# A causal convolution, GELU and two matrix products on one core: part of an operand sum goes to DMA, one more block takes Strassen's form

## The chip, the cores and the metric

The kernel runs on one core of a Trainium2 chip. Its engines work side by side and wait for each other by semaphores: TensorE (PE, with its weight loads as PEld), VectorE (DVE), ScalarE (ACT), GpSimd (POOL) and SyncE (SP, which here only issues DMAs). The metric is the device time of one execution in microseconds (us).

## What is computed

The input x has 8 sequences of 4096 tokens with 192 channels, 32768 tokens in all. Each of 8 heads (24 channels) has a causal filter of 7 taps, its weights put through a softmax. The result goes through a two-layer network with 2048 hidden channels and an exact GELU:

```python
w = softmax(weight)                                   # [8 heads, 7 taps]
y[b, s, h, :] = sum_k w[h, k] * x_pad[b, s + k, h, :] # 6 zeros ahead of each sequence
h = y @ w_in                                          # [32768, 192] @ [192, 2048]
out = gelu(h) @ w_out                                 # [32768, 2048] @ [2048, 192], float32
```

## The kernel before

**Tiling.** The tokens are cut into two halves of 16384, one on each half of the 128 partitions. A half is cut into 35 blocks, six of 256 tokens and then 29 of 512 (numbers 6 to 34); a block number stands for that block of both halves. Per block: SP loads x (`load`), DVE transposes it (`trans`, L705), DVE convolves it (`conv`, L726 and L733, with the first tap of some blocks on ACT, L848), PE makes the first product into PSUM (`mm1`, L972), ACT applies GELU into `gT` (L880), PE makes the second product (`mm2_t` L1050, or `mm2_s` L1110 for a Strassen block), the result is transposed by DVE into `osb` (`evac_t` L364, `st_evac` L517), and SP stores it (`store`, L547).

**Stages.** PE's loop over n runs the first product of block n in 16 slices, each of 12 matmuls, and after every slice a share of the second product of block n-1. Matmuls use 64x64 quarters of the array, four at a time; one such group of four with 512 columns is called a round here. A slice of the first product is 3 rounds, a block 48; the second product of a block is 48 rounds too. The first product goes into two PSUM buffers in turn (`hp`), so slice u waits for the GELU of slice u-2.

**Strassen blocks.** For every third block from 9 on (the list `ST`: 9, 12, ..., 30) the second product takes Strassen's form: the two halves of the tokens and pairs of hidden and output columns are a 2x2 matrix of blocks, and sums of operands replace products. It needs 44 rounds (`ROUNDS` says how many after each slice). Its sums of GELU outputs are S1, S3, Dn and S4 (`st_add`, DVE, L454 to L462), each in parts, held in `sst`; S3 is used by the product P7. `st_copy` (ACT, L482) copies partial results out of PSUM in six steps numbered 0 to 5, `st_post` (DVE, L491 to L505) makes five sums of them, `st_evac` transposes the three results. The sums of weights that the form needs are made once by `weights`, L426 to L436.

**What sets the order.** DVE's program is a list of convolution steps per block, with other work put in at places given as (blocks after m, step, order) in `AT_ST` and `at_ev`; DVE works on the convolution of block n+1 while PE is in the first product of block n. ACT's copies stand at (blocks after m, slice) in `AT_COPY`. All engines run their lists strictly in order. SP's loop is: load block n+3, then store block n-1, which waits for that block's last transpose. POOL, after the prologue, has only `halo`: it copies the last 6 tokens of a block ahead of the next block (L632); its DMAs are all in the prologue.

```python
AT_ST = {
    "S1": [(1, 9, 0), (2, 0, 0), (2, 1, 0), (2, 5, -1)],
    "S3": [(2, 0, 1), (2, 5, 1)],
...
AT_COPY = {0: (1, 6), 1: (1, 8), 2: (1, 10), 3: (1, 13), 4: (1, 14), 5: (2, 1)}
```

**The end.** The last block, 34, has no block after it: its second product runs by itself, in four groups g of two matmul chains (L1166). Even groups use PSUM banks that block 33 leaves free (`wait_banks`), odd groups the two `hp` buffers. `evac_half` (L336 on DVE, L338 on ACT) moves each result out, `store_half` stores it.

Of the kernel before, what the change touches and what calls it, by code (L numbers as in the profile page):

```python
# [5 lines left out]
ALU = mybir.AluOpType  # L6
# [5 lines left out]
def bass_lightweight_conv__then__act_gelu_exact_kernel(  # L12
# [58 lines left out]
    M0, M1 = 6, NB - 1  # L71
    ST = [m for m in range(M0 + 3, M1 - 1) if m % 3 == 0]
    K0 = {n: i for i, n in enumerate([4, 5, 6, *(n for n in range(9, NB) if n - 3 not in ST)])}
# [48 lines left out]
    with es:  # L122
# [64 lines left out]
        S_AC = sem("S_AC")  # L187
        S_DP = sem("S_DP")

        block = es.enter_context(nc.Block())  # L190
# [114 lines left out]
        def wait_banks(t, m, g):  # L305

            k = G0[m] + g
            if m < M0:
                if k >= 2:
                    t.wait_ge(S_EVA, k - 1)  # L310
            elif g % 2:
                t.wait_ge(S_GELU, SL0[NB] - 1 + g // 2)
            else:
                t.wait_ge(S_EV, EVC[M1] - 2 + g)
# [94 lines left out]
        def weights(v, k):  # L409

            def b(row, col):
                return ap(wout, row * C + col, [[NF * C, 128], [2 * C, NF // 2], [NP, 64]])

            full = [[NF // 2 * 64, 128], [64, NF // 2], [1, 64]]

            def w(i):
                return ap(wst, i * (NF // 2) * 64, [[4 * NF // 2 * 64, 128], [64, NF // 2], [1, 64]])

            f = ap(wtf, 0, full)
            if k == 0:  # L420
                for i in range(4):
                    v.wait_ge(S_WOUT[i], 16)
            else:
                v.wait_ge(S_WT, k)
            if k == 0:
                ins = v.tensor_tensor(f, b(0, 1), b(0, 0), ALU.subtract)  # L426
            elif k == 1:
                ins = v.tensor_copy(w(0), f)
            elif k == 2:
                ins = v.tensor_tensor(f, f, b(1, 1), ALU.subtract)  # L430
            elif k == 3:
                ins = v.tensor_copy(w(1), f)
            elif k == 4:
                ins = v.tensor_tensor(w(3), b(1, 0), f, ALU.add)
            else:
                ins = v.tensor_tensor(w(2), b(1, 1), b(0, 1), ALU.subtract)  # L436
            ins.then_inc(S_WT)

        PART = {"S1": 4, "S3": 2, "Dn": 2, "S4": 2}

        def st_add(v, m, name, q):
# [11 lines left out]
            if name == "S1":  # L453
                ins = v.tensor_tensor(t(0), a(1, 0), a(1, 1), ALU.add)  # L454
            elif name == "S3":
                ins = v.tensor_tensor(t(1), a(0, 0), a(1, 0), ALU.subtract)
            elif name == "Dn":
                v.wait_ge(S_SA[0], PART["S1"] * i + (q + 1) * n * PART["S1"] // (NF // 2))
                ins = v.tensor_tensor(t(2), a(0, 0), t(0), ALU.subtract)  # L459
            else:  # L460
                v.wait_ge(S_SA[2], PART["Dn"] * i + q + 1)
                ins = v.tensor_tensor(t(3), a(0, 1), t(2), ALU.add)  # L462
            ins.then_inc(S_SA[NS.index(name)])

        def st_copy(a, m, k):
# [6 lines left out]
            if k in (0, 1, 3):  # L472
# [4 lines left out]
                (p5s[LO, 0 : TB // 2], xb(UP, TB // 2)),  # L477
                (uu[LO, :], xb(LO)),
                (gsm[UP, :], uu[LO, :]),
                (uu[UP, :], uu[LO, :]),  # L480
            )[k]
            a.activation(out=dst, in_=src, func=AF.Copy).then_inc(S_AC)  # L482

        def st_post(v, m, k):
# [3 lines left out]
            if k == 0:  # L488
                st_done(v, m, "P7")
                v.wait_ge(S_AC, 6 * i + 2)  # L490
                ins = v.tensor_tensor(tq[UP, :], bank(BK[m]["Y"], UP), p5s[UP, :], ALU.add)  # L491
            elif k == 1:
# [6 lines left out]
            elif k == 3:  # L499
                v.wait_ge(S_AC, 6 * i + 6)  # L500
                v.wait_ge(S_DP, 5 * i + 3)
                ins = v.tensor_tensor(tq[:, :], tq[:, :], uu[:, :], ALU.add)
            else:
                v.wait_ge(S_MM2, MMC[m + 1])
                ins = v.tensor_tensor(gsm[:, :], bank(BK[m]["Y"]), gsm[:, :], ALU.add)  # L505
            ins.then_inc(S_DP)
# [24 lines left out]
        def store(e, m):  # L531
# [30 lines left out]
            "S1": [(1, 9, 0), (2, 0, 0), (2, 1, 0), (2, 5, -1)],  # L562
            "S3": [(2, 0, 1), (2, 5, 1)],
            "Dn": [(2, 0, 2), (2, 5, 2)],
            "S4": [(2, 0, 4), (2, 6, 0)],
            "post": [(2, 11, 0), (3, 0, 0), (3, 2, 0), (3, 6, 0), (3, 6, 1)],
            "ev": [(3, 6, 3), (3, 6, 2), (3, 4, 0)],
        }
# [6 lines left out]

        AT_COPY = {0: (1, 6), 1: (1, 8), 2: (1, 10), 3: (1, 13), 4: (1, 14), 5: (2, 1)}

        @block.gpsimd
        def _(g):
# [71 lines left out]
            halo(2)  # L651
            for n in range(3, NB):
                halo(n)

        @block.vector
        def _(v):
# [117 lines left out]
            for n in range(M0, M1):  # L774
# [3 lines left out]
                else:  # L778
                    for name, ats in AT_ST.items():
                        for q, at in enumerate(ats):  # L780
# [4 lines left out]
                            else:  # L785
                                todo.append((at, st_add, n, name, q))
                side += [((n + at[0], *at[1:]), op, v, *rest) for at, op, *rest in todo]
# [14 lines left out]
        def _(a):  # L802
# [52 lines left out]
            for n in range(NB):  # L855
                w = WS[n]
                for i in range(NSL[n]):
# [26 lines left out]
                    ).then_inc(S_GELU)  # L884

            for g in range(NG[NB - 1]):
                evac_half(a, g, 1)
                store_half(a, g, 1)

        @block.tensor  # L890
        def _(t):
# [182 lines left out]
            def mm2_s(m, e):  # L1074
# [18 lines left out]
                else:  # L1093
                    q = NS.index(src)
                    need(S_SA[q], PART[src] * i + k * PART[src] // (NF // 2) + 1)
                    a, c0 = sst[q], k * TB
# [123 lines left out]
```

## Time and profile before

| | |
|---|---|
| median of 3 runs | 674.67 us (674.18 to 674.76) |
| the profiled execution | 676.39 us, of which span 674.7 us |
| PE busy | 668.8 us (99%) |
| DVE busy | 605.7 us (90%) |
| ACT busy | 584.8 us (87%) |
| POOL busy | 33.1 us (5%) |
| DMA | 53.66 MB, mean 80 GB/s |
| granted PE clock | full speed in every slice of the span |

The span is what the profiler saw from the first to the last instruction; times inside it count from its start. Rows of the timeline give start, duration, engine, line, operation, the tile written and the tile read, shape and count; in square brackets stands how long the engine was idle before, and what ended that. Rows of the waits give who waited for whom, the total in us, how often, and the longest. Rows of a table of stretches give the stretch, its length, the busy time of PE, PEld, DVE, ACT and POOL with the number of instructions, the granted clock, the share of time that the DMA engines were busy, and GB/s. Rows of DMA issues give the number of DMAs, the size of each, and the median us from issue to landing.

### The profile page before, as it was taken

What the parts mean: (1) busy time and instruction counts of PE and PEld (TensorE: products, weight loads), DVE (VectorE), ACT (ScalarE), POOL (GpSimd) and SP (SyncE); (2) the same over time, 40 slices, a digit from 0 to 9 for tenths busy, and PEclk for the clock granted to TensorE, in tenths of its full rate; (3) what the DMA queues carried; (4) which work ended last, traced back from release to release, by engine and by line L of the source; (5) the groups of instructions that cost most, each with busy time, mean ns of one, the idle gap of its engine ahead of it and who ended that gap; (6) DMA issues with size and microseconds to landing.
All of it is one profiled execution on the core that took longest, in us unless ns stands there. A gap on an engine that the chain in (4) does not pass through costs nothing.

```text
span 674.7 us, 27139 instructions
## 1 busy us (share of the span) xinstructions
PE 668.8 (99%) x12504; PEld 418.6 (62%) x12504; DVE 605.7 (90%) x697; ACT 584.8 (87%) x653; POOL 33.1 (5%) x61
## 2 busy tenths in 40 slices
PE   8999999999999999999999999999999999999998
PEld 7999655556555555655565555556555655555557
DVE  5979999899999999999999999999999999998311
ACT  7899988889888988988898889888889988898773
POOL 7000000000000000000000000000000000000000
PEclk9999999999999999999999999999999999999999
DMA  8435234214443043433134431334431344411123
GB/s 146 115 85 142 60 73 90 63 41 96 96 96 81 20 94 96 96 83 85 33 88 96 95 88 22 89 92 95 94 86 31 80 96 95 89 28 47 32 50 94
DMA packets 133282, 53.66 MB, mean 80 GB/s; under 512 B 126384, under 2 KB 133104, under 8 KB 133168
## 3 DMA queue, kind: packets, MB, share of 16 engines
q1 hardware_dynamic: 129136, 49.37, 32.0%
q0 software_dynamic: 2912, 1.97, 2.0%
q8 instruction: 98, 1.61, 1.0%
q10 hardware_dynamic: 1120, 0.59, 0.3%
q14 instruction: 16, 0.13, 0.1%
HBM read 28.31 MB, written 25.17 MB: 79 GB/s over the span
## 4 chain that ended last, share of the span: by engine, by line
PE 93%; ACT 5%; DMA 1%; issue 0%; SPq 0%; DVE 0%; POOL 0%; POOLq 0%; ACTq 0%
PE hp L972 47%; PE ob L1050 31%; PE ob L1110 9%; PE ob L1012 5%; ACT gT L880 4%; DMA xin<-in_x_dram 1%; PE ob L1166 1%; PE hp L1166 1%; ACT gsm L482 1%; ACT uu L482 1%; PE ob L914 0%; DMA wsb<-in_weight_dram 0%; SPq L527 0%; PE ob L972 0%; POOL xTb L265 0%
## 5 line engine op out<-in xcount | busy, mean ns | idle before, releaser
L880 ACT ACTIVATE gT<-hp 128x1024 bf16<-128x1024 f32 x510 | 517.6, 1022 | 74.6 <-PE hp L972 67.7
L972 PE MATMUL hp<-xc,win 64*64 64x512 bf16 (+2 forms) x6036 | 417.6, 366 | 1.0
L733 DVE SCALAR_TENSOR_TENSOR acc<-xT,wcol,acc 128x1024 f32<-128x1024 f32 (+1 forms) x330 | 298.1, 959 | 10.8 <-ACT acc L848 10.8
L972 PEld LDWEIGHTS hp<-xc,win 64*64 64x64 bf16 (+1 forms) x6036 | 192.1, 106 | 128.2 <-ACT gT L880 4.9
L1050 PE MATMUL ob<-gT,wout 64*64 64x512 bf16 x3840 | 261.7, 376 | 0.0
L1050 PEld LDWEIGHTS ob<-gT,wout 64*64 64x64 bf16 x3840 | 123.5, 118 | 87.3
L1110 PE MATMUL ob<-gT,wout 64*64 64x512 bf16 x768 | 97.2, 376 | 0.0
L1110 PE MATMUL ob<-sst,wst 64*64 64x512 bf16 x384 | 79.1, 376 | 0.0
L364 DVE STREAM_TRANSPOSE osb<-ob 128x512 f32<-128x512 f32 x60 | 49.9, 872 | 32.5 <-PE ob L1050 32.5
L705 DVE STREAM_TRANSPOSE xT<-xin 128x1536 f32<-128x1536 f32 (+2 forms) x39 | 74.5, 1920 | 0.9 <-DMA xin<-in_x_dram 0.6
L733 DVE SCALAR_TENSOR_TENSOR xc<-xT,wcol,acc 128x1024 bf16<-128x1024 f32 (+1 forms) x66 | 61.9, 960 | 0.3
L1110 PEld LDWEIGHTS ob<-gT,wout 64*64 64x64 bf16 x768 | 43.5, 118 | 22.2
L632 POOL COPY xT<-xT 128x18 f32<-128x18 f32 x30 | 19.7, 655 | 508.9 <-DVE xc L733 284.7
L848 ACT ACTIVATE acc<-xT,wcol 128x512 f32<-128x512 f32 (+1 forms) x63 | 43.7, 693 | 0.0
L1012 PE MATMUL ob<-wout,gT 64*128 64x192 bf16 x768 | 41.6, 243 | 0.0
L1012 PEld LDWEIGHTS ob<-wout,gT 64*128 64x128 bf16 x768 | 34.2, 94 | 4.2
L1110 PEld LDWEIGHTS ob<-sst,wst 64*64 64x64 bf16 x384 | 32.2, 107 | 5.4
L1110 PE MATMUL ob<-gT,wst 64*64 64x512 bf16 x128 | 35.3, 376 | 0.0
L1110 PE MATMUL ob<-sst,wout 64*64 64x256 bf16 x256 | 27.4, 269 | 0.0
L454 DVE TENSOR_TENSOR sst<-gT 128x1024 bf16<-128x1024 bf16 x32 | 22.0, 688 | 5.4 <-ACT gT L880 5.4
L1110 PEld LDWEIGHTS ob<-sst,wout 64*64 64x64 bf16 x256 | 21.8, 119 | 2.1
L459 DVE TENSOR_TENSOR sst<-gT,sst 128x2048 bf16<-128x2048 bf16 x16 | 19.4, 1216 | 0.0
(73 smaller groups left out, 221.5 us busy)
## 6 DMA issues: line engine op xcount, KB each, us to landing
out_dram<-osb SPq DMA_DIRECT2D x124, 192.0 KB, 3.2
xin<-in_x_dram SPq DMA_DIRECT2D x116, 192.0 KB, 4.0
xin<-in_x_dram SPq DMA_DIRECT2D x18, 96.0 KB, 2.6
wout<-in_moe_w_out_dram POOLq DMA_DIRECT2D x4, 192.0 KB, 4.6
win<-in_moe_w_in_dram POOLq DMA_DIRECT2D x4, 96.0 KB, 4.5
win<-in_moe_w_in_dram POOLq DMA_DIRECT2D x2, 192.0 KB, 5.2
xin<-in_x_dram POOLq DMA_DIRECT2D x4, 96.0 KB, 4.4
out_dram<-osb ACTq DMA_DIRECT2D x4, 96.0 KB, 2.2
```

The source lines that it names most:

```text
L364: v.transpose(osb_t(m, j), bank(BK[m][j])).then_inc(S_EV)
L454: ins = v.tensor_tensor(t(0), a(1, 0), a(1, 1), ALU.add)
L459: ins = v.tensor_tensor(t(2), a(0, 0), t(0), ALU.subtract)
L632: g.tensor_copy(dst, src).then_inc(S_HALO)
L705: v.transpose(out, src).then_inc(S_TR)
L733: ins = v.scalar_tensor_tensor(dst, src, wk, a, op0=ALU.mult, op1=ALU.add)
L848: a.activation(out=acc[n % 2][:, p * TB : p * TB + w], in_=ap(xT[n % 2], p * XW + HX, [[NP * XW, 128], [1, w]]), func=AF.Copy, scale=wcol[ ...
L880: a.activation(out=ap(gT[n % 2], i * c * 2 * w, dst), in_=ap(ob, 2 * TB, [[4 * TB, 128], *src[1:]]) if u < SL0[1] and u % 3 == 2 else ap(h ...
L972: ins = t.matmul(hbuf(u, slice(fo, fo + fw), o, w), ap(win, f1, [[NP * F, 64], [2, fw]]), xc[n % 2][r, p * TB : p * TB + w], start=(p == 0 ...
L1012: ins = t.matmul(bb[sub], gT[m % 2][r, c0 : c0 + 128], wout[r, CH[sub][i] * C : (CH[sub][i] + 1) * C], start=(ph == 0 and k == 0), stop=(p ...
L1050: ins = t.matmul(bank(BK[m][j], slice(64 * h, 64 * h + 64), w), ap(wout, 64 * hf * NF * C + CH[h][i] * C + j, [[NF * C, 64], [NP, 64]],), ...
L1110: ins = t.matmul(bank(BK[m][bk], slice(64 * cg, 64 * cg + 64), w), wt_, a[r, c0 : c0 + w], start=(e == mine[0]), stop=(e in (mine[-1], GRO ...
```

## The change

Signs are changed so that S3 is a plain sum of two GELU outputs, a(0,0) + a(1,0). Three of its four quarters are then made by DMA, issued from POOL: a copy of the first operand within SBUF, and an accumulating DMA of the second operand on top. The copy of quarter q waits for the GELU slices that make it, the accumulate for the copy. The last quarter stays with DVE. The other signs (Dn, three of the weight sums, one of the sums after the product, the scale of ACT copies 4 and 5) follow from that. Copies 4 and 5 of ACT change their order and places, the last sums and transposes of a Strassen block move to later steps, and block 33 joins the Strassen list, with the waits of the last block's second product and of ACT's end set for it. In the diff, `M1` is 34.

```diff
-    ST = [m for m in range(M0 + 3, M1 - 1) if m % 3 == 0]
+    ST = [m for m in range(M0 + 3, M1) if m % 3 == 0]
...
+        S_CP = [sem("S_CP%d" % q) for q in range(3)]
+        S_AD = [sem("S_AD%d" % q) for q in range(3)]
...
         def wait_banks(t, m, g):
...
+            elif M1 - 1 in ST:
+                i = ST.index(M1 - 1)
+                t.wait_ge(*((S_AC, 6 * i + 4) if g == 0 else (S_EV, EVC[M1] - 2)))
+                t.wait_ge(S_DP, 5 * i + 3 + g)
             else:
                 t.wait_ge(S_EV, EVC[M1] - 2 + g)
...
         def weights(v, k):
...
-                ins = v.tensor_tensor(f, b(0, 1), b(0, 0), ALU.subtract)
+                ins = v.tensor_tensor(f, b(0, 0), b(0, 1), ALU.subtract)
...
-                ins = v.tensor_tensor(f, f, b(1, 1), ALU.subtract)
+                ins = v.tensor_tensor(f, f, b(1, 1), ALU.add)
...
-                ins = v.tensor_copy(w(1), f)
+                ins = v.tensor_scalar(w(1), f, -1.0, None, ALU.mult)
...
-                ins = v.tensor_tensor(w(3), b(1, 0), f, ALU.add)
+                ins = v.tensor_tensor(w(3), b(1, 0), f, ALU.subtract)
...
-                ins = v.tensor_tensor(w(2), b(1, 1), b(0, 1), ALU.subtract)
+                ins = v.tensor_tensor(w(2), b(0, 1), b(1, 1), ALU.subtract)
...
-        PART = {"S1": 4, "S3": 2, "Dn": 2, "S4": 2}
+        PART = {"S1": 4, "S3": 4, "Dn": 2, "S4": 2}
+        ND = 3
+
+        def st_dma(e, m, q, h):
+
+            i, n = ST.index(m), NF // 2 // PART["S3"]
+            dst = ap(sst[1], q * n * TB, [[NF // 2 * TB, 128], [TB, n], [1, TB]])
+            src = ap(gT[m % 2], (4 * q * n + h) * TB, [[NF * 2 * TB, 128], [4 * TB, n], [1, TB]])
+            if h == 0:
+                e.wait_ge(S_GELU, SL0[m] + 2 * (q + 1) * n - 1)
+                e.dma_start(dst, src).then_inc(S_CP[q], 16)
+            else:
+                e.wait_ge(S_CP[q], 16 * (i + 1))
+                e.dma_start(dst, src, accum_op=ALU.add).then_inc(S_AD[q], 16)
...
         def st_add(v, m, name, q):
...
-                ins = v.tensor_tensor(t(1), a(0, 0), a(1, 0), ALU.subtract)
+                ins = v.tensor_tensor(t(1), a(0, 0), a(1, 0), ALU.add)
...
-                ins = v.tensor_tensor(t(2), a(0, 0), t(0), ALU.subtract)
+                ins = v.tensor_tensor(t(2), a(0, 0), t(0), ALU.add)
...
         def st_copy(a, m, k):
...
-                (gsm[UP, :], uu[LO, :]),
                 (uu[UP, :], uu[LO, :]),
+                (gsm[UP, :], uu[LO, :]),
             )[k]
-            a.activation(out=dst, in_=src, func=AF.Copy).then_inc(S_AC)
+            a.activation(out=dst, in_=src, func=AF.Copy, scale=-1.0 if k > 3 else 1.0).then_inc(S_AC)
...
         def st_post(v, m, k):
...
-                ins = v.tensor_tensor(tq[UP, :], bank(BK[m]["Y"], UP), p5s[UP, :], ALU.add)
+                ins = v.tensor_tensor(tq[UP, :], bank(BK[m]["Y"], UP), p5s[UP, :], ALU.subtract)
...
-                v.wait_ge(S_AC, 6 * i + 6)
+                v.wait_ge(S_AC, 6 * i + 5)
                 v.wait_ge(S_DP, 5 * i + 3)
...
                 v.wait_ge(S_MM2, MMC[m + 1])
+                v.wait_ge(S_AC, 6 * i + 6)
...
-            "S3": [(2, 0, 1), (2, 5, 1)],
+            "S3": [(2, 5, 1)],
...
-            "post": [(2, 11, 0), (3, 0, 0), (3, 2, 0), (3, 6, 0), (3, 6, 1)],
-            "ev": [(3, 6, 3), (3, 6, 2), (3, 4, 0)],
+            "post": [(2, 11, 0), (3, 0, 0), (3, 2, 0), (3, 6, 0), (3, 9, 0)],
+            "ev": [(3, 10, 0), (3, 7, 0), (3, 4, 0)],
...
-        AT_COPY = {0: (1, 6), 1: (1, 8), 2: (1, 10), 3: (1, 13), 4: (1, 14), 5: (2, 1)}
+        AT_COPY = {0: (1, 6), 1: (1, 8), 2: (1, 10), 3: (1, 13), 4: (2, 1), 5: (2, 4)}
...
         @block.gpsimd
         def _(g):
...
-            for n in range(3, NB):
-                halo(n)
+            for n in range(3, M1 + 2):
+                if n < NB:
+                    halo(n)
+                if n - 2 in ST:
+                    for q, h in ((0, 0), (1, 0), (0, 1), (2, 0), (1, 1), (2, 1)):
+                        st_dma(g, n - 2, q, h)
...
         @block.scalar
         def _(a):
...
+            for k, (d, at) in AT_COPY.items():
+                if NB - d in ST:
+                    st_copy(a, NB - d, k)
...
             def mm2_s(m, e):
...
-                    need(S_SA[q], PART[src] * i + k * PART[src] // (NF // 2) + 1)
+                    part = k * PART[src] // (NF // 2)
+                    if src == "S3" and part < ND:
+                        need(S_AD[part], 16 * (i + 1))
+                    elif src == "S3":
+                        need(S_SA[q], i + 1)
+                    else:
+                        need(S_SA[q], PART[src] * i + part + 1)
```

More of the change, by code (lines that the diff above doesn't have):

```diff
@@ L478, in st_copy @@
                 (uu[LO, :], xb(LO)),
+                (uu[UP, :], uu[LO, :]),
                 (gsm[UP, :], uu[LO, :]),
-                (uu[UP, :], uu[LO, :]),
             )[k]
-            a.activation(out=dst, in_=src, func=AF.Copy).then_inc(S_AC)
+            a.activation(out=dst, in_=src, func=AF.Copy, scale=-1.0 if k > 3 else 1.0).then_inc(S_AC)
         def st_post(v, m, k):
@@ L785, in _ @@
                             else:
-                                todo.append((at, st_add, n, name, q))
+                                todo.append((at, st_add, n, name, q if name != "S3" else ND))
                 side += [((n + at[0], *at[1:]), op, v, *rest) for at, op, *rest in todo]
```

## The prediction

> **What bounds the kernel now.** I read the page's busy times first, then the table of stretches with one row per block, then the list of waits, then ScalarE's timeline where PE waits, then the DMA issues.
>
> ```profile
> PE 668.8 (99%) x12504; PEld 418.6 (62%) x12504; DVE 605.7 (90%) x697; ACT 584.8 (87%) x653; POOL 33.1 (5%) x61
> ```
>
> PE is the bound. A block is 96 rounds of four 64x64 tiles (48 for the first product, 48 for the second), a Strassen block 92. The stretches below begin at first-product slice 0 of blocks 9, 10, 11 and 12; block 9 is in Strassen's form, so its second product runs in the second row.
>
> ```profile
> 127.05:147.77 20.72, 20.72 (x389) 11.83 (x384) 20.04 (x24) 17.89 (x20) 0.20 (x1) 1.00 0.35 78
> 147.77:167.92 20.15, 20.04 (x388) 12.27 (x380) 19.92 (x21) 18.41 (x22) 0.72 (x1) 1.00 0.36 81
> 167.92:188.67 20.75, 20.75 (x386) 11.80 (x389) 20.05 (x23) 18.46 (x21) 1.19 (x1) 1.00 0.35 79
> 188.67:209.39 20.72, 20.72 (x390) 11.77 (x385) 20.03 (x24) 17.89 (x20) 0.20 (x1) 1.00 0.33 78
> ```
>
> Columns: stretch, its length, then busy time of PE, weight loads, DVE, ACT, POOL, granted clock, DMA share. A round is 20.72/96 = 0.2158 us, the clock is full, and 92 rounds should take 19.86. The Strassen stretch took 20.15 and the next 20.75: 0.29 + 0.03 = 0.32 us lost per Strassen block. The waits name the loser, and the timeline the place.
>
> ```profile
> DVE acc L733 <- ACT acc L848: 10.8, 14, 2.4
> DVE sst L454 <- ACT gT L880: 5.4, 8, 0.7
> PEld hp L972 <- ACT gT L880: 4.9, 9, 0.6
> ```
>
> ```profile
> 164.68 0.58 ACT L482 ACTIVATE uu<-ob 64x512 f32<-64x512 f32 x1
> 165.16 1.01 ACT L880 ACTIVATE gT<-hp 128x1024 bf16<-128x1024 f32 x1
> 166.19 0.63 ACT L482 ACTIVATE gsm<-uu 64x512 f32<-64x512 f32 x1
> 166.84 3.00 ACT L880 ACTIVATE gT<-hp 128x1024 bf16<-128x1024 f32 x3
> ...
> 167.92 0.36 PEld L972 LDWEIGHTS hp<-xc,win 64*64 64x64 bf16 x12 [0.59 <-ACT gT L880]
> ```
>
> Two copies on two successive slices push the GELUs back until PE finds its PSUM buffer still unread at 167.92. The 0.59 includes the gap that weight loads have anyway; the loss is the 0.32. DVE, at about 60.0 us in the 61.62 us of three blocks, is nearly full but ahead: block 12's convolution ends at 183.30 and PE wants it at 188.67.
>
> **The change part by part.** The sum goes against the profiled execution (676.39 us, span 674.7); its time is 1.72 over the median 674.67, and I carry the difference over to the median.
>
> *The moved ScalarE copy.* Copies 4 and 5 of a Strassen block leave slice 14 of the next block and slice 1 of the one after for slices 1 and 4 of the one after, at 0.63 each, and swap their order. In the first of the two, without the copy at 14, GELU 14 runs 166.17 to 167.19 and PE wants slice 0 of the next block 5 rounds (3 of slice 15, 2 of the second product) after 166.56, at 167.64: 0.45 to spare, the stall goes. What is late next? The copy at slice 1 runs 169.55 to 170.18, GELU 1 ends 171.25, PE wants slice 3 at 171.55: 0.30 spare, as now (0.29). The copy at slice 4 makes GELU 4 end 175.13 against slice 6 at 175.65: 0.5 spare. So 8 x 0.32 = 2.5 us are gained. DVE's op that needs copy 4 stood at 170.57, 0.4 after the copy; late, it would cost DVE tenths out of its 5.4 us lead.
>
> *Block 33 in Strassen's form.* 20.72 - 19.86 = 0.86 us gained, in the last first-product stage, with the copies placed as above. Behind it, in old times: the last GELU ends 662.23, two copies end 663.5, ScalarE's first eviction waited until 664.37 anyway. DVE does 0.69 + 0.89 + 0.69 of sums and transpose from 662.9, so the Y bank is read by 665.2; PE's third final group, which now waits for it, started at 666.81: 1.6 spare. The last transpose ends 665.9 instead of 663.2, SP's four stores follow until 668.3, and the last output is evicted at 672.29. Nothing on the path.
>
> *DVE work removed.* Two 128x2048 sums per Strassen block (1.20 each) become one 128x1024 (0.69, by the row of that shape): 1.72 us less. DVE is off the path: worth 0 to PE. The weights' signs change, six operations as before; the scale of -1 on a copy changes no operation's shape.
>
> *The six transfers per Strassen block*, three copies and three accumulates of 256 KB, SBUF to SBUF, on POOL's queue. Before shows no such transfer. POOL's queue stands still in these waits; behind them is only the halo copy of block m+3. The one of block 12, at 137.87 now, would come near 148; the transpose that needs it runs at 165.27: 17 us of cover. The last copy waits for the 11th GELU (142.34), the last accumulate for that copy; PE needs the third quarter at round 12 of the Strassen stretch, 153.60. The nearest rows are POOL's own transfers:
>
> ```profile
> wout<-in_moe_w_out_dram POOLq DMA_DIRECT2D x4, 192.0 KB, 4.6
> win<-in_moe_w_in_dram POOLq DMA_DIRECT2D x4, 96.0 KB, 4.5
> win<-in_moe_w_in_dram POOLq DMA_DIRECT2D x2, 192.0 KB, 5.2
> out_dram<-osb ACTq DMA_DIRECT2D x4, 96.0 KB, 2.2
> ```
>
> They ran with the DMA engines 0.80 busy. Here the queues are empty until the next stores:
>
> ```profile
> 142.30:150.90 8.60, 8.60 (x168) 4.90 (x160) 8.60 (x11) 7.65 (x9) 0.00 (x0) 1.00 0.01 3
> ```
>
> At 4.6 each: copy landed 147.0, accumulate landed 151.6, 2.0 us before PE asks. At 5.2: 152.8, 0.8 before. The accumulate has no row. Lower end: 2.2, no loss either way (it can't gain, PE waits for nothing else there). Upper end: twice 5.2, since it reads two operands: from 147.0 it lands at 157.4, 3.8 us late, nine times 34 us. I take 4.6 to 5.2, nearest by queue and size, so no loss. Loss starts at an accumulate of 6.6 us.
>
> [...]
>
> Could POOL's six issues (about 0.7 each) hold DVE? A 64x768 DVE copy took 0.58 beside an issue and 0.42 without: six cost 1.0. The other end, each blocking DVE fully: 4.2. I take 1.0: DVE at 60.0 - 1.7 + 1.0 = 59.3 in 61.30.
>
> *Output transposes spread out.* The last one of a Strassen block moves behind four convolution steps, ending near 177.1 instead of 173.4. SP's store waits for it, and the load queued behind that store moves too: landing 183.3 becomes 187.0, and the transpose that wants it at 185.83 waits 1.2 us on DVE. Its convolutions end at 199.4 and 222.9, PE wants them at 209.4 and 229.5: hidden by over 6 us. Without that lead it would cost 1.2 x 8. The sum that frees the Y bank moves with them, from 171.9 to about 175.6; the bank's next writer is the second product of block 11, from 188.7. The one wait more per quarter on PE (three DMA semaphores and one of DVE's in place of two) I cost at nothing: rounds that wait on semaphores now keep the 0.2158 step.
>
> Sum: 2.5 + 0.86 = 3.4 us off; 676.4 becomes 673.0 profiled, 674.7 becomes **671.3** as median.
>
> **The rivals.**
> 1. *The accumulate lands late* (slower). Place: the third quarter's wait at round 12. It decides from a landing of 7.0 us, where (7.0 - 6.6) x 9 eats the gain. At 7.5, halfway from 4.6 to the upper end, 8.1 lost: 679.4. For: two operands, one queue in order. Against: idle DMA engines. 0.14.
> 2. *The stall only moves*: ScalarE, one copy more in the following block, stalls PE by as much as before, and only block 33 counts: 673.8, within 0.2%. For: 0.30 us spare at slice 3. Against: that is what is spare today. 0.10.
> 3. *DVE becomes the bound*: each issue blocks it fully, 60.0 - 1.7 + 4.2 = 62.5 against 61.30, 1.2 x 8 = 9.6 lost: 680.9. Against: the 0.58 beside 0.42. 0.05.
>
> **How the numbers follow.** Measurement tells about 0.2% (1.35 us) from no change: faster is under 673.3, slower over 676.0. The forecast has 0.71 and its own range 670.4 to 672.6 (a spare time misjudged by 0.1 us, eight times, and 0.4 at the tail). Faster 0.71, same 0.10, slower 0.14 + 0.05 = 0.19. The range begins at 670.3 and takes in rival 2 and an accumulate of up to 7.3 us: 671.3 + 0.7 x 9 = 677.6. Past it lie most of rival 1 and rival 3, and 2 or 3 in 100 of the forecast: under 2 in 10.
>
> **What would show it.** Right: the Strassen stretch at 19.9, its follower at 20.7, no wait of weight loads on GELU with 0.6; a last first-product stage of 19.9; the accumulates landing under 6.6 us after issue; DVE near 58 to 59 us per three blocks. Wrong: PE waiting for a DMA into the sum buffer some four slices into the Strassen stretch; DVE rows grown beside POOL issues; a new wait on GELU at slice 3 or 6 of the following block.

## The result, and the profile after

| | before | after |
|---|---|---|
| median of 4 runs each, on one chip | 674.42 us (673.85 to 674.76) | 670.93 us (670.6 to 671.28) |
| ratio, 95% interval | | 0.9949 (0.9932 to 0.9966) |
| the profiled execution | 676.39 us, span 674.7 us | 670.93 us, span 669.2 us |

The kernel became 3.5 us faster; 3.4 was forecast. The two profiled spans differ by 5.5 us, more than the medians, because the prologues of these two executions differ: the first product of block 6 begins at 69.85 in the one and at 67.72 in the other, 2.13 us that are no part of the change. What remains lies in two places. The eight cycles of three blocks from the first slice of block 9 on took 492.92 us and now take 490.45: 2.47 us. The stage of the last first product, block 34 beside the second product of block 33, took 20.83 and now takes 19.97: 0.86 us. The stretches between are equal, and the tail behind that stage is 13.1 us long in both. In this document, medians and ratios leave out executions over 1.5% slower than the fastest of the same kernel: one of 1007.15 us (mean clock 0.66) of the kernel with the transfers alone, and two, of 732.5 and 735.0, of the kernel whose third copy waits for all 16 GELUs, whose trace is of the first of these two.

The page of the changed kernel: busy times, the chain that ended last, three groups.

```profile
PE 665.8 (99%) x12504; PEld 416.2 (62%) x12504; DVE 604.7 (90%) x703; ACT 587.8 (88%) x659; POOL 91.9 (14%) x115
...
PE 99%; ACT 0%; DVE 0%; DMA 0%; issue 0%; ACTq 0%
...
L652 POOL COPY xT<-xT 128x18 f32<-128x18 f32 x30 | 28.9, 964 | 330.9 <-DVE xc L757 171.3
...
L455 POOL DMA_DIRECT2D sst<-gT x27 | 19.8, 733 | 175.1 <-ACT gT L904 175.1
...
L458 POOL DMA_DIRECT2D sst<-gT x27 | 33.1, 1227 | 8.0 <-DMA sst<-gT 7.9
```

PE alone makes the chain now. In the three groups, POOL spends 0.73 us on issuing a copy and 1.23 on issuing an accumulate, and its halo copies, 0.655 us each before, take 0.964.

The table of stretches of the changed kernel: blocks 9 to 12 one by one, the three blocks from 9 on together, and the last first-product stage. The columns are as in the prediction: length, busy time of PE, weight loads, DVE, ACT and POOL, granted clock, DMA share, GB/s.

```profile
124.92:145.64 20.72, 20.72 (x389) 11.77 (x384) 19.80 (x23) 17.89 (x20) 6.21 (x7) 1.00 0.73 147
145.64:165.50 19.86, 19.86 (x388) 12.28 (x384) 18.50 (x21) 17.90 (x21) 0.72 (x1) 1.00 0.41 90
165.50:186.22 20.72, 20.72 (x388) 11.77 (x384) 19.84 (x23) 19.04 (x22) 1.19 (x1) 1.00 0.34 79
186.22:206.94 20.72, 20.72 (x388) 11.77 (x384) 20.39 (x24) 17.89 (x20) 6.23 (x7) 1.00 0.71 147
...
124.92:186.22 61.30, 61.30 (x1156) 35.82 (x1152) 58.14 (x65) 54.82 (x61) 8.12 (x9) 1.00 0.50 105
...
636.09:656.06 19.97, 19.97 (x388) 12.16 (x381) 6.62 (x9) 18.01 (x21) 0.00 (x0) 1.00 0.22 50
```

The Strassen stretch is 92 rounds of 0.2158 us, 19.86, with nothing lost; its follower is 20.72. DVE has 58.14 us of work in the 61.30 of the three blocks.

ScalarE's timeline of the changed kernel, across the place where PE used to stall:

```profile
161.63 1.02 ACT L904 ACTIVATE gT<-hp 128x1024 bf16<-128x1024 f32 x1 [0.27 <-PE hp L999]
162.55 0.58 ACT L501 ACTIVATE uu<-ob 64x512 f32<-64x512 f32 x1
163.02 2.00 ACT L904 ACTIVATE gT<-hp 128x1024 bf16<-128x1024 f32 x2
165.29 2.10 ACT L904 ACTIVATE gT<-hp 128x1024 bf16<-128x1024 f32 x2 [0.27 <-PE hp L999]
167.42 0.63 ACT L501 ACTIVATE uu<-uu 64x512 f32<-64x512 f32 x1
...
171.31 0.63 ACT L501 ACTIVATE gsm<-uu 64x512 f32<-64x512 f32 x1
```

Only one copy is left among the last slices of the Strassen stretch. The two GELUs behind it end at 165.02, PE begins the next block at 165.50: 0.48 us to spare, where PE used to wait. The two later copies stand at 167.42 and 171.31; PE's slices 3 and 6 of that block then have 0.29 and 0.50 us to spare.

The waits of the changed kernel that replaced the one on GELU (of which one of 0.2 us is left), and the row of DMA issues for the new transfers:

```profile
DVE xT L729 <- DMA xin<-in_x_dram: 9.3, 8, 1.9
POOL sst L458 <- DMA sst<-gT: 7.9, 9, 1.3
DVE acc L757 <- ACT acc L872: 7.3, 12, 1.8
```

```profile
sst<-gT POOLq DMA_DIRECT2D x54, 256.0 KB, 4.1
```

DVE waits for a load eight times, 1.2 us each on average; PE waits for none of it. The last issues of block 9's transfers on POOL's timeline of the changed kernel:

```profile
140.51 0.73 POOL L455 DMA_DIRECT2D sst<-gT  x1 [3.44 <-ACT gT L904]
141.22 1.25 POOL L458 DMA_DIRECT2D sst<-gT  x1
143.26 1.19 POOL L458 DMA_DIRECT2D sst<-gT  x1 [0.79 <-DMA sst<-gT]
144.00 0.83 POOL L652 COPY xT<-xT 128x18 f32<-128x18 f32 x1
```

The third quarter's copy, issued at 140.51, landed 2.46 us later by the semaphore it sets; the accumulate was issued at 143.26 and landed at 148.88. PE asks for it at 151.47: 2.6 us to spare. Over the nine blocks this accumulate took 3.6 to 5.6 us, median 3.9; the 5.6 of block 9 is the longest, the next is 4.2.

### The profile page after: what moved, and what is told of

Its sections match the earlier page's. It is cut to its first block, busy times and chain, and to the rows that moved or that the text cites. A ratio compares the mean times of both kernels' runs of the same rounds, so it can differ in the third digit from the quotient of the medians.

```text
span 669.2 us, 27224 instructions
## 1 busy us (share of the span) xinstructions
PE 665.8 (99%) x12504; PEld 416.2 (62%) x12504; DVE 604.7 (90%) x703; ACT 587.8 (88%) x659; POOL 91.9 (14%) x115
## 4 chain that ended last, share of the span: by engine, by line
PE 99%; ACT 0%; DVE 0%; DMA 0%; issue 0%; ACTq 0%
PE hp L999 49%; PE ob L1077 29%; PE ob L1143 13%; PE ob L1039 5%; PE ob L1199 1%; PE hp L1199 1%; PE ob L941 0%; DMA wsb<-in_weight_dram 0%; PE ob L999 0%; ACT dg L846 0%; DVE wcol L701 0%; ACT xc L237 0%; DVE wnm L692 0%; ACT osb L344 0%; ACT wex L833 0%
## 5 line engine op out<-in xcount | busy, mean ns | idle before, releaser
L1143 PE MATMUL ob<-sst,wst 64*64 64x512 bf16 x432 | 88.9, 376 | 0.0
L652 POOL COPY xT<-xT 128x18 f32<-128x18 f32 x30 | 28.9, 964 | 330.9 <-DVE xc L757 171.3
L370 DVE STREAM_TRANSPOSE osb<-ob 128x512 f32<-128x512 f32 x57 | 47.6, 874 | 4.0 <-PE ob L1077 3.7
L455 POOL DMA_DIRECT2D sst<-gT x27 | 19.8, 733 | 175.1 <-ACT gT L904 175.1
L1143 PEld LDWEIGHTS ob<-sst,wst 64*64 64x64 bf16 x432 | 36.2, 107 | 6.0
L1143 PE MATMUL ob<-gT,wst 64*64 64x512 bf16 x144 | 39.7, 376 | 0.0
L458 POOL DMA_DIRECT2D sst<-gT x27 | 33.1, 1227 | 8.0 <-DMA sst<-gT 7.9
L473 DVE TENSOR_TENSOR sst<-gT 128x1024 bf16<-128x1024 bf16 x36 | 24.9, 691 | 10.0 <-ACT gT L904 9.9
L1143 PE MATMUL ob<-sst,wout 64*64 64x256 bf16 x288 | 30.8, 269 | 0.0
```

The lines of the kernel that those rows point to most:

```text
L370: v.transpose(osb_t(m, j), bank(BK[m][j])).then_inc(S_EV)
L458: e.dma_start(dst, src, accum_op=ALU.add).then_inc(S_AD[q], 16)
L652: g.tensor_copy(dst, src).then_inc(S_HALO)
L1143: ins = t.matmul(bank(BK[m][bk], slice(64 * cg, 64 * cg + 64), w), wt_, a[r, c0 : c0 + w], start=(e == mine[0]), stop=(e in (mine[-1], GRO ...
```

## The experiments

The theory at first was that of the prediction: moving the copy removes a stall of 0.32 us eight times, block 33 gives 0.86, and the transfers give PE nothing since DVE is off the path. The rivals were that the transfers carry part of the gain (DVE being closer to the bound than its lead suggests), and that the transfers cost something. Each ratio below is against the kernel before, run on the same chip; the medians come from several chips, on which the kernel before had 674.42 to 674.67. Where two profiled executions are compared from block 6 to the end, it is to leave out the prologue, which differs from one execution to the next by up to 2.7 us.

### The transfers alone

The changed kernel with block 33 taken out of the list and everything else at the old places: only the six transfers per Strassen block and the signs remain.

```diff
-    ST = [m for m in range(M0 + 3, M1) if m % 3 == 0]
+    ST = [m for m in range(M0 + 3, M1 - 1) if m % 3 == 0]
...
-            "post": [(2, 11, 0), (3, 0, 0), (3, 2, 0), (3, 6, 0), (3, 9, 0)],
-            "ev": [(3, 10, 0), (3, 7, 0), (3, 4, 0)],
+            "post": [(2, 11, 0), (3, 0, 0), (3, 2, 0), (3, 6, 0), (3, 6, 1)],
+            "ev": [(3, 6, 3), (3, 6, 2), (3, 4, 0)],
...
-        AT_COPY = {0: (1, 6), 1: (1, 8), 2: (1, 10), 3: (1, 13), 4: (2, 1), 5: (2, 4)}
+        AT_COPY = {0: (1, 6), 1: (1, 8), 2: (1, 10), 3: (1, 13), 4: (1, 14), 5: (2, 1)}
```

> The kernel before with one part of the change alone: S3's three quarters by transfers and the signs that go with them; copies 4 and 5 (in their new order), sums, transposes and the Strassen list at the old places. My theory: DVE busy falls to near 58 in three blocks, nothing else moves: 674.4 as before, within 0.6, Strassen stretch 20.15. Rival, the relief is worth something by itself: 672 or less, stretch nearer to 19.86. Other rival, POOL's issues hold up DVE: above 675.

Measured: 674.39 us, ratio 0.9995 (0.9986 to 1.0004). The stall is where it was; from its list of waits:

```profile
PEld hp L999 <- ACT gT L904: 4.9, 9, 0.6
```

DVE's work in three blocks fell from 60.0 to 58.6 us and PE's cycle stayed at 61.62. By themselves the transfers cost nothing and give nothing.

### The copies back at their old places

The changed kernel with only the line of `AT_COPY` put back.

> The changed kernel with ScalarE copies 4 and 5 back at slice 14 of the next block and slice 1 of the one after; all else as changed. My theory: the stall comes back, 0.32 in each of eight Strassen stretches and about 0.3 in block 33's, 2.9 us: 673.8 (673.2 to 674.4), Strassen stretch 20.15, weight loads waiting on GELU with 0.6 each. Rival, the copy was not the cause and the relief of DVE took the stall away: 670.9, stretch 19.86.

Measured: 673.73 us, 0.9987 (0.9977 to 0.9997). The wait on GELU returns with the same 4.9 us in 9, and the stretches with 20.15 and 20.75. With the transfers in place, the new places of the copies are worth 673.73 - 670.93 = 2.8 us (604.06 - 601.48 = 2.6 in the profiled executions, from block 6 to the end).

### Without block 33

Only the first line of the diff above.

> The changed kernel with block 33 left in the normal form. My theory: 92 rounds become 96 once, 0.86 us: 671.8 (671.2 to 672.4), last first-product stage 20.7 to 20.8 where it is 19.9. Rival, the longer tail behind block 33 (two copies, five sums, later store) eats it: 670.9 or less.

Measured: 671.77 us, 0.9954 (0.9941 to 0.9966): block 33 is worth 0.84 us by the medians. The two intervals overlap, but the traces agree: 602.34 us from block 6 to the end against 601.48, 0.86 more, all of it in the stage of the last first product.

### S3 made by DVE again

The changed kernel without its transfers: DVE makes S3 in two halves, as before. Copies, sums, transposes and block 33 stay at their new places.

```diff
-        PART = {"S1": 4, "S3": 4, "Dn": 2, "S4": 2}
+        PART = {"S1": 4, "S3": 2, "Dn": 2, "S4": 2}
...
-            "S3": [(2, 5, 1)],
+            "S3": [(2, 0, 1), (2, 5, 1)],
...
-                if n - 2 in ST:
-                    for q, h in ((0, 0), (1, 0), (0, 1), (2, 0), (1, 1), (2, 1)):
-                        st_dma(g, n - 2, q, h)
```

> The changed kernel with S3 made by DVE alone, in two halves as before; copies 4 and 5, the sums and transposes and block 33 as changed. My theory: the transfers only relieve DVE, which is not on the path, so the time stays at that of the changed kernel, 670.9 (670.3 to 671.6), Strassen stretch 19.86, three blocks 61.30, DVE busy near 59.9 of them (58.14 + 1.72). Rival, the relief of DVE is what makes room: DVE with 59.9 busy and the waits it has now (some 3 us) no longer fits into 61.30; first-product stages wait for the convolution, three blocks take 62 or more, and the time is 677 or above.

Measured: 673.34 us, 0.9975 (0.9965 to 0.9986), where neither said it would be. Four of its eight cycles (length, then busy times as above), and its waits:

```profile
247.37:308.68 61.31, 61.31 (x1156) 38.76 (x1151) 59.52 (x66) 54.60 (x61) 4.17 (x3) 1.00 0.35 80
308.68:370.76 62.08, 61.71 (x1160) 42.57 (x1157) 60.49 (x66) 54.98 (x61) 4.78 (x3) 1.00 0.37 78
370.76:432.44 61.68, 61.53 (x1157) 42.61 (x1152) 59.98 (x66) 54.80 (x61) 4.77 (x3) 1.00 0.37 79
432.44:494.27 61.83, 61.52 (x1156) 42.48 (x1152) 60.61 (x66) 54.78 (x61) 2.02 (x3) 1.00 0.36 79
```

```profile
DVE xT L726 <- DMA xin<-in_x_dram: 9.5, 8, 1.5
...
PEld ob L1135 <- DVE tq L510: 3.1, 6, 0.9
```

The first three cycles run at 61.30; DVE's convolutions of blocks 11, 14 and 17 end 6.3, then 6.1, then 5.8 us ahead of PE, and in every later cycle it is 5.8 again. From the fourth cycle on PE waits for a sum after the product (L510), which DVE makes between the last two steps of these convolutions and now makes too late:

```profile
343.33 0.10 PEld L1135 LDWEIGHTS ob<-gT,wst 64*64 64x64 bf16 x1 [0.85 <-DVE tq L510]
```

So the room that DVE had was not the 4.5 us and more by which its convolutions are ahead. It was that of this sum, and there the kernel before had 0.2 us left between the sum's end, at 160.53, and the weight load that needs it:

```profile
159.84 0.69 DVE L491 TENSOR_TENSOR tq<-ob,p5s 64x512 f32<-64x512 f32 x1
160.74 0.11 PEld L1110 LDWEIGHTS ob<-gT,wst 64*64 64x64 bf16 x1
```

Here it is 0.2 us too in the first cycle, in the changed kernel 0.8. PE bore a delay of some half a microsecond, from 6.3 to 5.8, before it lost time. The transfers do matter, then, but only together with the copies. The next run tests that alone.

### The copies and the spread sums alone

The kernel above, and block 33 out of the list.

> The kernel before with the moved copies and the spread sums and transposes alone (and the signs): S3 by DVE, block 33 normal. Theory: what the copy gives at first is lost to DVE later, as with block 33 in Strassen's form: 0.86 more than the kernel with S3 by DVE and block 33, 674.2 (673.4 to 674.8), that is 0.3 gained. Rival, the copy is worth its 2.5 us by itself: 672.0.

Measured: 674.53 us, 0.9991 (0.9980 to 1.0002). Four versions without block 33 then make a square:

| no block 33 | copies and last sums at the old places | at the new places |
|---|---|---|
| S3 by DVE | 674.6 (the kernel before) | 674.53 |
| three quarters of S3 by transfers | 674.39 | 671.77 |

By these medians each alone gives nothing that can be told from 0; both together give 2.8 us. The profiled executions, from block 6 to the end, say nearly the same: 604.81 before, 604.82 with the transfers, 604.22 with the copies and sums, 602.34 with both. So the copies and sums alone may keep up to 0.6 of their 2.5 us. Two things have changed for DVE: with PE's stall gone a cycle of PE takes 61.30 us instead of 61.62, and the spread transposes bring a wait for a load.

### Loads one block earlier

The wait for the load is 1.2 us per cycle: a store waits for the spread transposes, and a load is queued behind it. Here S3 stays with DVE, block 33 stays in, and SP issues each load one block earlier.

```diff
+            load(sp, 4)
             for n in range(1, NB):
-                if n + 3 < NB:
-                    load(sp, n + 3)
+                if n + 4 < NB:
+                    load(sp, n + 4)
                 store(sp, n - 1)
```

> The kernel with S3 by DVE alone, copies, transposes and block 33 as changed, and SP issuing each load one block earlier (load n+4 ahead of store n-1), so that the transpose after the spread output transposes waits for no load. Theory now: without the transfers DVE's own cycle of three blocks is about 61.7 (59.9 to 60.5 busy, 1.2 to 1.5 of it waiting for that load), over the 61.30 of PE, its lead runs out after some four cycles and PE waits for the first sum after the product; without the load wait the cycle is some 60.5, PE is the bound again, all cycles 61.30: 671.0 (670.4 to 671.8). Rival, DVE's busy time and its other waits are too much by themselves: 673 or more, with PE waiting for that sum in the later cycles.

Measured: 671.59 us, 0.9954 (0.9942 to 0.9967). One of its cycles, and its only wait for loads, a single one:

```profile
309.50:370.81 61.31, 61.31 (x1158) 35.80 (x1153) 60.09 (x66) 54.78 (x61) 2.10 (x3) 1.00 0.35 79
```

```profile
DVE xT L726 <- DMA xin<-in_x_dram: 3.5, 1, 3.5
```

All eight cycles are 61.30 or 61.31, with DVE busy for 60.1 of it (59.2 in the last) and no transfer of S3 at all. From block 6 to the end it takes 601.5 us, as the changed kernel does. So DVE's work does fit into the shorter cycle, and it is the work and the load's wait together that don't. How they would do in the longer cycle no run shows.

### Sums packed again, S3 by DVE

Was the load the only thing DVE could not afford? The kernel with S3 made by DVE, and the last sums and transposes back at step 6, where no load waits.

> The sum S3 made wholly by DVE in two halves, the copies of ACT at their new places, block 33 in Strassen's form, the last sums and transposes of a Strassen block packed at step 6 as in the kernel before. It asks whether the wait for the load that the spread transposes cause (1.2 us per three blocks) was the only reason why the version with DVE making S3 came to 673.3. Theory: no, DVE is short of time whichever way: packed, its last sum stands for copy 5 of ACT instead (20.9 us in 8 waits, 2.6 per cycle, in the version with the transfers), its busy time of about 59.3 per cycle goes up to about 62 against PE's 61.30, so after its lead is used up every cycle is about 62 long: 672.5 to 677, a wait of PE on the first sum after the product in several cycles, no loads waited for. Rival: the spread alone was to blame; packed, the kernel reaches what the changed kernel has, 670.9 to 671.5, with cycles of 61.30 throughout.

Measured: 682.22 us, 1.0117 (1.0100 to 1.0134), slower than before. Two cycles, and two waits:

```profile
186.15:248.96 62.81, 62.13 (x1158) 38.70 (x1154) 60.04 (x66) 54.83 (x61) 4.78 (x3) 1.00 0.36 78
248.96:311.83 62.87, 62.03 (x1156) 41.59 (x1152) 60.11 (x66) 54.83 (x61) 4.17 (x3) 1.00 0.35 78
```

```profile
DVE gsm L525 <- ACT gsm L501: 20.7, 8, 2.9
PEld ob L1135 <- DVE tq L510: 8.2, 7, 1.2
```

DVE stands 2.6 us per cycle for the later copy 5 instead, and its cycle, not PE's, sets the time from the second one on. The theory held in its mechanism; its 677 as upper end was too low by 5 us.

### Sums packed again, with the transfers

The changed kernel with only the sums and transposes back at step 6.

> The changed kernel with the last sums and transposes of a Strassen block back at their old steps, in one piece after the sixth convolution step; copies 4 and 5 stay in the next block but one. Theory: DVE stands some 2.5 us until copy 5 ends (slice 4), in place of the load wait, out of a lead of 5 us: 670.9 (670.3 to 671.6). Rival, the wait on the copy eats the room that the transfers made, and PE waits for the first sum after the product in later cycles: 672 or more.

Measured: 670.94 us, 0.9946 (0.9932 to 0.9961), as the changed kernel. The wait for copy 5 is the same:

```profile
DVE gsm L525 <- ACT gsm L501: 20.9, 8, 2.9
...
PEld ob L1143 <- DVE tq L510: 1.5, 5, 0.4
```

Here DVE can just afford it. It uses up its room, though: the convolutions that ended 6.95 us ahead of PE in the first cycle end 5.8 ahead from the fourth on, and PE begins to wait for the sum. A budget puts all of these runs on one line: DVE's mean work per cycle, plus the wait that returns in each cycle, against PE's 61.30.

| version | DVE's work | its returning wait | together | mean cycle seen |
|---|---|---|---|---|
| after | 58.5 | 1.2, load | 59.7 | 61.31 |
| S3 by DVE, early loads | 60.0 | none | 60.0 | 61.31 |
| after, sums packed | 58.2 | 2.6, copy 5 | 60.8 | 61.34 |
| S3 by DVE | 60.0 | 1.2, load | 61.2 | 61.52 |
| S3 by DVE, no block 33 | 59.9 | 1.3, load | 61.2 | 61.54 |
| S3 by DVE, sums packed | 60.05 | 2.55, copy 5 | 62.60 | 62.83 (from the second on) |

Work is the busy time of DVE over the eight cycles divided by eight (in the last row, of the seven from the second on), waits are the totals divided by eight (10.0 us for the version without block 33; in the last row, the mean of the same seven cycles). Up to 60.8 PE sets the cycle, from 61.2 DVE does. On top come gaps of at most 0.1 us between DVE's operations, 0.2 to 0.3 per cycle in every version, which take 61.2 past 61.30. Where DVE sets the pace they close the sum: 62.60 + 0.22 in the last row, and in the cycle of 62.08 us shown above, with S3 by DVE, 60.49 of work, 1.35 of the wait for the load and 0.24 of such gaps. (The other rows with S3 by DVE and the load's wait are means over cycles of both kinds.) Where PE sets the pace, the rest of DVE's time goes into waits for ACT. With S3 by DVE and early loads they are, in the cycle shown above:

```profile
DVE sst L473 <- ACT gT L901: 0.7, 1, 0.7
DVE acc L754 <- ACT acc L869: 0.3, 1, 0.3
```

This 1.0 us is all that a returning wait may take there, and the load's takes 1.2 on average and up to 1.5.

### Early loads on top of the changed kernel

> The changed kernel with SP issuing each load one block earlier. Theory: the transfers already leave DVE room, so the 9.3 us that DVE waits for loads go and PE gains nothing: 670.9 (670.3 to 671.6), stretch 19.86, three blocks 61.30. Rival, DVE is still near enough to the bound that PE gains: under 670.3.

Measured: 671.09 us, 0.9955 (0.9938 to 0.9971). DVE's eight waits for loads shrink to one of 2.2 us, and PE gains nothing: with the transfers DVE has time enough. From block 6 to the end both kernels take 601.48 us.

### How far the transfers are from costing something

Two runs push the accumulate later. In the first, all four quarters of S3 go by DMA. The fourth needs the last GELUs of the block, so its accumulate is issued beside the stores.

```diff
-        ND = 3
+        ND = 4
...
-            "S3": [(2, 5, 1)],
+            "S3": [],
...
-                    for q, h in ((0, 0), (1, 0), (0, 1), (2, 0), (1, 1), (2, 1)):
+                    for q, h in ((0, 0), (1, 0), (0, 1), (2, 0), (1, 1), (2, 1), (3, 0), (3, 1)):
```

> The changed kernel with the last quarter of S3 by copy and accumulate too. Theory: its copy waits for the 15th GELU (145.4), lands at 147.9, the accumulate is issued at 148.2 and lands 3.9 to 5.6 later, at 152.1 to 153.8; PE wants it at round 14, 152.55: between no stall and 1.3 us in each Strassen stretch, 671 to 682, most likely 675. Rival, accumulates stay at 3.6 as in the last cycles: 670.9 or less.

Measured: 700.77 us, 1.0377 (1.0351 to 1.0404), well past the forecast. Its stretches around the first such place, PE's timeline there, and its waits:

```profile
145.50:170.00 24.50, 21.69 (x385) 14.08 (x381) 17.65 (x19) 18.13 (x21) 3.77 (x4) 0.93 0.49 99
...
154.00:156.00 2.00, 0.00 (x0) 0.00 (x0) 2.00 (x3) 0.26 (x1) 0.00 (x0) 1.00 1.09 232
156.00:158.00 2.00, 1.80 (x20) 1.06 (x24) 0.92 (x1) 0.59 (x1) 0.00 (x0) 0.59 1.23 237
158.00:160.00 2.00, 2.00 (x30) 1.60 (x25) 0.00 (x0) 1.02 (x1) 0.00 (x0) 0.56 0.48 76
160.00:162.00 2.00, 2.00 (x45) 1.32 (x37) 0.00 (x0) 1.47 (x2) 0.00 (x0) 1.00 0.00 0
```

```profile
153.02 0.38 PE L1143 MATMUL ob<-gT,wout 64*64 64x512 bf16 x1
156.20 0.51 PE L1143 MATMUL ob<-sst,wst 64*64 64x512 bf16 x1 [2.81 <-DMA sst<-gT]
...
158.23 0.63 PE L1143 MATMUL ob<-sst,wst 64*64 64x512 bf16 x1
```

```profile
PEld ob L1143 <- DMA sst<-gT: 24.8, 9, 3.6
```

The accumulate was issued at 149.74, beside the stores (the DMA share is 1.09 in the row from 154 on), and landed at 156.16, 6.4 us later (median of the nine 6.35). PE stood still for 2.81 us, and the stretch became 24.50 - 19.86 = 4.6 us longer. The rest is the clock: in the two rows from 156 to 160 it is granted at 0.59 and 0.56, which is half speed for 3.4 us ((0.41 + 0.44) x 2 / 0.5), and the same matmul took 0.63 instead of 0.38. That didn't happen each time: the mean clock of the whole span, 0.988, makes 16.8 us at half speed (0.012 x 700.5 / 0.5), about five times 3.4, beside nine stalls. In all PE stood still for 20.5 us and 30.8 were lost (632.27 against 601.48 from block 6 to the end).

In the second, three quarters stay with the transfers, but the third quarter's copy waits for 16 GELUs instead of 11.

```diff
-                e.wait_ge(S_GELU, SL0[m] + 2 * (q + 1) * n - 1)
+                e.wait_ge(S_GELU, SL0[m] + (16 if q == 2 else 2 * (q + 1) * n - 1))
```

> The changed kernel with the copy of S3's third quarter waiting for all 16 GELUs of its block in place of 11. Theory (the third quarter has a deadline at round 12 of the Strassen stretch, 151.47 in the trace of the changed kernel): copy issued at 146.5, landed at 149.0, accumulate issued at 149.3 beside the stores, landed 3.9 to 5.6 later, at 153.2 to 154.9: PE stalls 1.7 to 3.4 in each Strassen stretch, nine times, 15 to 31 us: 686 to 702. Rival, PE has other slack there: 671 to 675.

Measured: 722.97 us, 1.0716 (1.0686 to 1.0745). This kernel's stretch of blocks 9 and 12, a part of the second, and the wait:

```profile
146.37:171.37 25.00, 21.97 (x388) 14.09 (x384) 18.30 (x20) 17.85 (x21) 4.20 (x5) 0.93 0.46 97
...
212.81:240.10 27.29, 22.46 (x390) 13.28 (x386) 18.63 (x20) 18.02 (x21) 4.19 (x5) 0.87 0.42 89
...
223.00:227.00 4.00, 2.95 (x28) 1.27 (x32) 1.41 (x2) 0.56 (x1) 0.00 (x0) 0.50 0.97 201
```

```profile
PEld ob L1143 <- DMA sst<-gT: 44.4, 18, 4.6
```

The mechanism is the expected one, but its size was missed in two terms: the accumulates took 6.3 us (median; 5.5 to 7.1) where 3.9 to 5.6 had been expected, again beside stores, and the clock was granted at half (0.50 in the row from 223 on): by the clocks of the two stretches for about 3.5 us in the first (0.07 x 25.00 / 0.5) and about 7.1 in the second (0.13 x 27.29 / 0.5), and by the mean clock of 0.960 for some 58 us of the span of 730.7.

### One Strassen block more

A try at something faster than both: the changed kernel with early loads and block 32 in Strassen's form too, right ahead of block 33. Its edit is the list and the waits that two such blocks in a row need on shared buffers:

```diff
-    ST = [m for m in range(M0 + 3, M1) if m % 3 == 0]
+    ST = sorted({m for m in range(M0 + 3, M1) if m % 3 == 0} | {M1 - 2})
...
+            if (q, h) == (0, 0) and m - 1 in ST:
+                st_done(e, m - 1, "P7")
...
+            if k == 0 and m - 1 in ST:
+                a.wait_ge(S_EV, EVC[m])
...
```

> The changed kernel with early loads and one Strassen block more, block 32, right before block 33, with the waits that two such blocks in a row need (sum buffers, copies, banks). Theory: a Strassen block is worth 4 rounds, 0.86 us, where DVE has room, and behind the last convolutions it has: 670.1 (669.4 to 670.9), the stretch of block 33's first product 19.9. Rival, the operand sums of block 33 come late, since they wait for those of block 32 to be used: a stall of 1 us or more in the last first-product stage, 671 or above.

Measured: 675.04 us, 1.0001 (0.9988 to 1.0014). The 0.86 that one block gives is lost in one wait, in the stretch of block 33's first product, which was to take 19.9 us:

```profile
PEld ob L1154 <- DVE sst L479: 3.2, 1, 3.2
```

```profile
617.73:640.59 22.86, 20.09 (x389) 13.56 (x385) 21.14 (x27) 17.72 (x21) 4.68 (x5) 1.00 0.42 100
```

Block 32's sums come at a point of the cycle where DVE has just made those that belong to block 30, and its convolution of block 33 ends 4.4 us ahead of PE; that of the block behind every earlier Strassen block ends 9.9 ahead. PE's weight load waits 3.2 us for one of the sums. The stretch is 3.0 us too long and the next one, of 20.3, is 0.3 longer than in the changed kernel: 670.1 + 3.3 = 673.4. That is where five of the twelve executions lie, 673.4 to 674.0, with the clock at full. The profiled one, of 675.81, has full clock too, but its block 6 begins 2.4 us later than that of the changed kernel. The other six, 674.9 to 676.7, have a mean clock of 0.997, which is worth 0.003 x 674 = 2.0 us. No trace of these six was kept, so that this stall is what halves their clock is likely and not shown. No version that was run beats the changed kernel by more than can be measured.

## Why the prediction was right, and where not

The time was right (670.93 against 671.3, within the likeliest case's range of 670.4 to 672.6), but one step of it was wrong, and this case didn't let it show.

- **The moved copy.** Forecast 8 x 0.32 = 2.5 us; the eight cycles became 2.47 shorter, and putting the copies back costs 2.8 (2.6 in the traces). The spare times held too: 0.48 at the next block's first slice (forecast 0.45), 0.29 at slice 3 (0.30), 0.50 at slice 6 (0.5). Rival 2, that the stall only moves, would have shown at slice 3, and 0.29 was enough.
- **Block 33.** Forecast 0.86; taking it out costs 0.84 (0.86 in the traces). Behind it the tail kept its length, as the prediction had worked out.
- **The transfers' cost.** The accumulate landed in 3.9 us (median), where 4.6 to 5.2 had been taken from other transfers of POOL's queue, and left PE 2.6 us in block 9, where 0.8 to 2.0 were forecast. The third quarter's copy, taken at the same 4.6 to 5.2, landed in 2.45 to 2.47 us in all nine blocks; in block 9 DVE was busy for the whole of it. Rival 1, the late accumulate, was a real mechanism, as two runs showed: issued beside the stores, an accumulate took 6.3 (median). But the rival priced a microsecond of stall at one: with the halved clock, which the prediction left out, a stall of 2.81 cost 4.6. The upper end given for the accumulate, 10.4, was not reached in any run.
- **POOL's issues and DVE.** Forecast 59.3 us of DVE's work in three blocks, measured 58.5 on average: 1.5 less than before's 59.95, most of the 1.72 that the arithmetic removes, so the six issues cost DVE some 0.3 and not 1.0, if all of the difference is theirs. Rival 3's blocking isn't there. An accumulate's issue takes 1.23 on POOL, not 0.7; it is inside the landing times above.
- **The step that failed: "DVE is off the path: worth 0 to PE".** And, of the same kind, that the late load is "hidden by over 6 us". Two things were wrong in it. First, the lead was read at the convolutions, which end 5 to 10 us ahead of PE. The nearest place where PE waits for DVE is the first sum after the product, and there 0.2 us were left. Second, a delay of 1.2 us was held against the lead as if it came once. It comes in every cycle, and what counts then is whether DVE's work, its returning wait and its small gaps fit into PE's cycle, which the change makes 0.32 us shorter. Without the transfers they don't fit (60.0 + 1.2 to 1.5 + 0.25 against 61.30), and of the copy's 2.5 us at most 0.6 would have been left, with 674.53 as the median. The 1.5 us by which DVE's work shrank, counted at 0, are what lets the copy's gain through. That the sum came out right is luck in this respect: it gave to the copy alone what the two parts give together, and both are in the change. The prediction's remark that the late load would cost 1.2 x 8 "without that lead" had the right term and took the lead to last. The run with early loads shows that it is the wait and the sums together: with the wait gone, DVE can make all of S3 itself at 671.59.

## What to carry to other kernels

When a stall of the bounding engine goes, its cycle gets shorter for all the others, and what was moved for it can bring them new waits. Add up the second-busiest engine's work, its returning waits and its small gaps per cycle and compare that with the new cycle, not with the old one. Read its lead at every place where the bounding engine waits for it and take the smallest: here it was 0.2 us at a sum, beside 5 to 10 at the convolutions. A lead covers a delay that happens once; a delay that returns in every cycle and doesn't fit uses it up, and the loss shows only some cycles later (here from the second or the fourth on). And a part of a change that gives nothing by itself may still carry the gain of another, so parts should be tried alone and together.

## What the hardware showed that was not expected

- A 256 KB accumulate within SBUF, issued last in its block with no load or store in flight, took 3.6 to 4.2 us from issue to landing in eight of nine blocks of the changed kernel and 5.6 in the first, for a reason that was not found; beside the stores it took 6.3 (median). A copy of the same size, also with no load or store beside it, took 2.46. The DMA share in the slow places was 0.9 to 1.2.
- TensorE's clock was granted at half after a stall of 2.81 us, for 3.4 us (all four quarters by DMA). But a stall of about that length doesn't always do it: in the profiled execution with block 32 PE stood still for 2.77 us (it was busy for 3.23 of the 6 us from 620 on) and the clock stayed at 1.00. Executions of one kernel differ in this: the four with all four quarters by DMA have mean clocks of 0.988 to 0.995, and of the twelve with block 32 six have 1.00 and six 0.997. What separates the stalls that are followed by half clock from the others was not shown. Shorter stalls, before's 0.32 us and the 0.7 that is PE's longest wait with S3 by DVE and packed sums, left the clock at 1.00 in these two traces.
- POOL's small halo copies went from 0.655 to 0.964 us each. In the run with S3 by DVE and packed sums, which has no such transfers at all, three of them take 4.78 us in the first of the two cycles shown, 1.59 each, so it isn't the transfers alone that slow them; what does was not pursued.
